# A third output row buffer, an earlier release of one weight load, and a range check moved to another place in the stream

## The chip, the cores and the metric

The kernel runs on one core of a Trainium2 chip. A core has a matrix engine (PE), whose weight loads are listed apart (PEld), a vector engine (DVE), an activation engine (ACT), a general engine (POOL) and a queue engine (SP) that mostly issues transfers. Every engine works through its own instructions in order and waits for the others by semaphores. The metric is the time of one execution in microseconds on the device, the median of several runs. A profile comes from one execution of its own.

## The reference

A gated linear attention is followed by a gated state-space layer with an output product. B, H, S, D are 4, 8, 768, 48; the model width is 384, the inner width 512.

```python
# attention, for every batch and head
for t in range(S):
    state = alpha[:, :, t, :, None] * state + einsum('bhd,bhe->bhde', k[:, :, t], v[:, :, t])
    y[:, :, t] = einsum('bhd,bhde->bhe', q[:, :, t], state)
# x: the heads side by side, (4, 768, 384)
proj = x @ w_in                       # w_in is 384 x 1024, float64 in memory
val, gate = proj[..., :512], proj[..., 512:]
for t in range(S):
    h = exp(A_log)[0] * h + val[:, t, :]      # one factor per channel in the kernel
    ys[:, t, :] = h
out = (gate * sigmoid(gate) * ys) @ w_out     # w_out is 512 x 384, float64 in memory
```

## The kernel before

The 4 x 768 steps are cut into N = 12 groups of 256, three to a batch. The kernel has two ways to compute: `fast`, which holds for inputs in a certain range, and `general`, which is correct for all. `fast` checks the range as it goes and leaves the last output product to a branch: if the check is good, the short last block (lines 1256 to 1270) makes that product, otherwise `general` starts over.

The order of the work in `fast` is written out by hand: there is no scheduler, and every engine takes its instructions in the order of the code.

The attention of a group m has these steps. `turn` or `turned` brings the raw rows of alpha, q, k into the layout needed; `scan_P` and `scan_V` make running products of alpha (DVE); `scaled_q` and `scaled_k` multiply; `scores` (PE, L792), `masks` (DVE L802 or L807, ACT, POOL); `values` (PE, L826 or, for the first group, L910), `states` (PE, L858), `carried` (PE, L839), and `join`, which copies the result out of PSUM and moves it by small transfers into xT. `first(m)` stands for scores and masks, `second(m)` for values across, states and sums, `third(m)` for carried, values and join.

The layer behind it has four projections for a group n, `project(n, cc)` with cc from 0 to 3: twelve matmul passes on PE (L976), a scan on DVE over the value half as soon as that half is there (L983), a Silu on ACT over the gate half (L994), and a product f on POOL, or on DVE in the first two and the last group (L996). Then `output(n)`: sixteen passes on PE (L1010) into two banks, of which the first is whole after fourteen; ACT copies each bank into an SBUF tile `o_sb` (L1004) taken from the pool `rows`, and SP issues its transfer to `out` (L1005). The pool has two buffers before. It belongs to the outermost function, and the last block takes its two tiles (L1267, L1269) from it as well.

The loop turn n does the projections of group n, the attention of group m = n + 1, and `output(n)` at its end. From n = 2 on, a turn's order is: `second(m)`, four projections, `third(m)`, `first(m + 1)` (there is none in turn 10, the attention being done), `output(n)`. The last turn, 11, has the four projections only, then all engines load the flag of the range check (L1234) and take the branch (L1255). A hint for the branch's target is given just before.

The weights come as float64 words and are converted on the chip. `w_in` is in four units of two transfers of 384 KB, one for each cc; `w_out` in two halves. For a unit i, `low(i)` (ACT, L543) takes the low word, `high(i)` (DVE, L549 and L551) the high word, `add_low(i)` (POOL, L556) joins them; `convert(i)` is the three together. PE's projection cc needs unit cc converted. Ahead of the loop the loads are held back by small instructions that write one element of their target: the load must wait for that write. For unit 1 it is a `memset` of DVE (L1059) that stands behind `high(0)`; for the loads after it (alpha of group 2, unit 2, and so on) it is a small copy of ACT (L1068). SP issues all of them in order.

The range check has these parts. `check_w(i)` makes the largest and the smallest absolute value of the high words of unit i (two reductions on DVE, L567), for i from 0 to 5: four units of `w_in`, two halves of `w_out`. `check_end()` (L574 to L583) turns these and the attention's own limits into one number for each partition, `okc`. `check_flag()` adds them over the partitions with a matmul into the bank s0 (L587), compares the sum (L589) and writes the integer `flag` (L590).

In turn 10 (n == N - 2), units 0 and 1 are checked behind the second projection, unit 2 behind the third, units 3 to 5 and the check's end behind `third(m)`. `check_flag()` stands in turn 11 behind the third projection.

## Time and profile before

| what | us |
|---|---|
| median of 3 runs | 276.58 |
| lowest and highest | 276.08, 277.28 |
| the profiled execution | 276.15 |
| its span, first to last instruction | 274.4 |

| engine | busy, us | share of the span |
|---|---|---|
| PE, matmul | 269.5 | 98% |
| PEld, weight loads | 216.9 | 79% |
| DVE | 217.7 | 79% |
| ACT | 109.6 | 40% |
| POOL | 123.8 | 45% |

The granted clock of PE was 1.00. A row of a timeline has the start and the length in us, the engine, the line of the kernel, the operation, output <- input, the shape, a count, and in brackets the idle time of the engine just before with what ended it. In a row of the chain of waits stand start, length and the work. Matmuls are pipelined and their ends are modelled, so the start of what waits for them is the surer mark. A letter q behind an engine's name (SPq, PEldq) is its sequencer: issues of transfers, loads of registers.

### The profile page before, as it was taken

Reading aid. Unit: us, or ns where it says so; the run is one execution under the profiler, and the core shown is the slowest. Engines: PE = TensorE matmul, PEld = TensorE weight load, DVE = VectorE, ACT = ScalarE, POOL = GpSimd, SP = SyncE. Lnnn points to the kernel's source line nnn. Section 1 sums busy time; section 2 is a strip of 40 time slices with the busy share of each in tenths; the row PEclk is TensorE's granted clock in tenths of the full one; section 3 lists DMA queues with packets and bytes.
Section 4 is the critical chain, followed back from the end, with each engine's and each line's share of the span. In section 5 each row is a group of like instructions: output and inputs, shape, how many; then the busy total and the mean of one; then the engine's idle time right before and its main releaser. Section 6 shows DMA issues by size and latency. Waiting matters only on the chain.

```text
span 274.4 us, 9649 instructions
## 1 busy us (share of the span) xinstructions
PE 269.5 (98%) x4060; PEld 216.9 (79%) x4060; DVE 217.7 (79%) x271; ACT 109.6 (40%) x252; POOL 123.8 (45%) x144
## 2 busy tenths in 40 slices
PE   8999999999999999999999999999999999999995
PEld 6988888877788687788688688688687787786874
DVE  6979998996798999694995995996995992179440
ACT  3668766451344333523434424425425415213211
POOL 8122223260137485385384485376366476325000
PEclk9999999999999999999999999999999999999999
DMA  6937985989639686774677595586596501201101
GB/s 188 319 113 221 304 182 160 256 172 230 168 92 227 163 189 152 199 170 116 153 183 155 149 210 136 142 202 144 137 210 146 137 0 36 70 0 42 63 5 60
DMA packets 52303, 41.18 MB, mean 150 GB/s; under 512 B 27392, under 2 KB 50944, under 8 KB 52256
## 3 DMA queue, kind: packets, MB, share of 16 engines
q1 hardware_dynamic: 49328, 37.34, 54.2%
q0 software_dynamic: 1536, 2.20, 2.9%
q10 hardware_dynamic: 1392, 0.99, 1.2%
q8 instruction: 33, 0.54, 0.9%
q14 instruction: 14, 0.11, 0.1%
HBM read 32.54 MB, written 4.72 MB: 136 GB/s over the span
## 4 chain that ended last, share of the span: by engine, by line
PE 91%; DVE 5%; issue 1%; ACT 1%; POOL 1%; DVEq 0%; POOLq 0%; ACTq 0%
PE mm L976 46%; PE mm L1010 21%; PE y L826 4%; PE y L839 4%; PE mm L792 3%; PE s L792 3%; PE s L858 3%; PE mm L1262 2%; DVE P L635 2%; PE mm L701 1%; PE y L773 1%; DVE V L654 1%; POOL w_in L556 1%; PE s L717 1%; DVE Zk L619 0%
## 5 line engine op out<-in xcount | busy, mean ns | idle before, releaser
L976 PE MATMUL mm<-xT,w_in 128*128 128x256 f32 x576 | 129.7, 382 | 0.1
L976 PEld LDWEIGHTS mm<-xT,w_in 128*128 128x128 f32 x576 | 107.9, 190 | 16.2 <-POOL w_in L556 0.4
L1010 PE MATMUL mm<-w_out,f_last 128*128 128x384 f32 x160 | 54.2, 492 | 0.0
L994 ACT ACTIVATE sg<-mm 128x256 f32<-128x256 f32 x48 | 18.4, 383 | 86.1 <-PE mm L976 86.0
L996 POOL TENSOR_TENSOR f_last<-sg,hh 128x256 f32<-128x256 f32 x36 | 33.0, 918 | 33.5 <-ACT sg L994 17.7
L1010 PEld LDWEIGHTS mm<-w_out,f_last 128*128 128x128 f32 x160 | 29.7, 190 | 19.8
L878 POOL TENSOR_TENSOR sum<-sum,dS 128x192 f32<-128x192 f32 x30 | 30.3, 1010 | 21.5 <-ACT dS L866 11.8
L983 DVE TENSOR_TENSOR_SCAN hh<-a_dec,hh,mm 128x256 f32<-128x256 f32 x32 | 23.4, 731 | 16.1 <-PE mm L976 16.1
L635 DVE TENSOR_TENSOR_SCAN P<-al,lower 128x1028 f32<-128x1028 f32 x12 | 31.4, 2618 | 0.5
L654 DVE TENSOR_TENSOR_SCAN V<-al,ends 128x1028 f32<-128x1028 f32 x12 | 28.3, 2360 | 0.4
L955 POOL DMA_DIRECT2D xT<-yst x44 | 22.5, 517 | 12.5 <-ACT yst L952 11.2
L1004 ACT ACTIVATE o_sb<-mm 128x384 f32<-128x384 f32 x22 | 10.8, 490 | 37.3 <-issue 21.2
L810 POOL TENSOR_TENSOR AK<-AK,mask 128x512 f32<-128x512 f32 x9 | 15.2, 1684 | 18.7 <-ACT AK L808 18.7
L807 DVE TENSOR_TENSOR A<-s,mask 128x256 f32<-128x256 f32 x9 | 3.8, 425 | 19.5 <-PE s L792 19.5
L556 POOL TENSOR_TENSOR w_in<-w_in,wr 128x768 int32<-128x768 int32 x4 | 7.3, 1822 | 25.9 <-DVE wr L551 16.1
L600 DVE STREAM_TRANSPOSE k<-raw_k 128x1024 f32<-128x1024 f32 x9 | 18.3, 2035 | 0.0
L600 DVE STREAM_TRANSPOSE q<-raw_q 128x1024 f32<-128x1024 f32 x9 | 18.2, 2021 | 0.0
L600 DVE STREAM_TRANSPOSE al<-raw_a 128x1024 f32<-128x1024 f32 x8 | 16.3, 2038 | 0.0
L619 DVE TENSOR_TENSOR Zk<-k,V 128x1024 f32<-128x1024 f32 (+1 forms) x14 | 16.1, 1150 | 0.1
L826 PEld LDWEIGHTS y<-AK,v 64*64 64x64 f32 x352 | 12.1, 134 | 5.1 <-issue 5.1
L610 DVE TENSOR_TENSOR Zq<-q,P 128x1024 f32<-128x1024 f32 (+1 forms) x14 | 14.8, 1060 | 0.1
L826 PE MATMUL y<-A,v 64*64 64x64 f32 x352 | 14.5, 221 | 0.0
(163 smaller groups left out, 389.7 us busy)
## 6 DMA issues: line engine op xcount, KB each, us to landing
v<-in_v_dram SPq DMA_DIRECT2D x22, 192.0 KB, 3.3
out_dram<-o_sb SPq DMA_DIRECT2D x22, 192.0 KB, 2.2
raw_k<-in_k_dram SPq DMA_DIRECT2D x18, 184.0 KB, 3.7
raw_q<-in_q_dram SPq DMA_DIRECT2D x18, 184.0 KB, 3.8
raw_k<-in_k_dram SPq DMA_DIRECT2D x18, 176.0 KB, 3.9
raw_q<-in_q_dram SPq DMA_DIRECT2D x18, 176.0 KB, 4.0
wbits<-in_moe_w_in_dram SPq DMA_DIRECT2D x8, 384.0 KB, 5.3
raw_a<-in_alpha_dram SPq DMA_DIRECT2D x16, 184.0 KB, 4.9
```

The lines of the kernel that those rows point to most:

```text
L600: nc.vector.transpose(out=by_runs(to).rearrange("p h c j -> p h j c"), in_=raws[name][:, 0:4 * ROW].rearrange("p (h j d) -> p h j d", h=4, ...
L635: nc.vector.tensor_tensor_scan(out=P, data0=al[:, 0:4 * GP], data1=lower.rearrange("p h t -> p (h t)"), initial=0.0, op0=ALU.mult, op1=ALU ...
L654: nc.vector.tensor_tensor_scan(out=V[:, ::-1], data0=al[:, 1:4 * GP + 1][:, ::-1], data1=ends.rearrange("p h t -> p (h t)")[:, ::-1], init ...
L792: nc.tensor.matmul(scs[m][c][i][ds(L * h, L), ds(p * (L + D), L + D)], Zk[rows, c, p, ds(h * L, L)], Zq[rows, u, p], start=True, stop=True ...
L826: nc.tensor.matmul(ys[m][i][ds(64 * s, 64), e, ds(c * C + h * L, L)], v_sb[rows, c, 4 * i + p, :], As[i][rows, c, p, :], start=across and ...
L878: nc.gpsimd.tensor_add(Ss[j][:, :, 0:D], Ss[j - 1][:, :, 0:D], part)
L955: engines[n % len(engines)].dma_start(out=xT[to, a], in_=st[rows, i, e])
L976: nc.tensor.matmul((pv, pg)[vg], w_ins[cc][:, kk, vg, :], xT[:, kk, :], start=(kk == 0), stop=(kk == NK - 1))
L983: nc.vector.tensor_tensor_scan(out=hh, data0=a_dec[:, cc:cc + 1].to_broadcast([C, GC]), data1=pv, initial=prev_h[cc][:, GC - 1:GC] if n % ...
L994: nc.scalar.activation(sg, pg, AF.Silu)
L996: f = lambda: engine.tensor_mul(fs[n][cc], sg, hh)
L1010: nc.tensor.matmul(os[c], fs[n][cc][:, ds(c * C, C)], w_outs[cc // 2][:, cc % 2, :], start=(cc == 0), stop=(cc == NI - 1))
```

## The change

There are three edits.

1. The pool `rows` has three buffers in place of two.
2. The `memset` that holds the load of unit 1, and the load's two transfers on SP, stand ahead of `low(0)` and `high(0)`, right behind `masks(0)`. On DVE the memset now precedes the two instructions of `high(0)`; on SP the order of issues is the same.
3. The parts of the range check stand elsewhere. In turn 10, units 0 to 3 are checked ahead of the first projection's scan, unit 4 behind the second, unit 5 behind the third, and the check's end behind the fourth. `check_flag()` comes at the end of turn 10 ahead of `output(10)`: on PE its matmul stands between the last matmuls of `third(11)` (L839) and the first of `output(10)` (L1010), and on DVE the two instructions of the flag precede the scans of turn 11.

The number of instructions is the same on every engine. The waits that are built into them differ in a few places: the copies into `o_sb` wait for a transfer one output further back, and L587 now has a wait for DVE (okc).

```diff
@@ ahead of the loop
     masks(0)
+    nc.vector.memset(wbits[units[1]][0:1, 0, 0, 0:1, 0], 0)
+    load_w(units[1], nc.sync)
     low(0)
     high(0)
-    nc.vector.memset(wbits[units[1]][0:1, 0, 0, 0:1, 0], 0)
-    load_w(units[1], nc.sync)
     add_low(0)
@@ the loop, n of 2 and more
+            if n == N - 2:
+                for i in range(4):
+                    check_w(i)
             f0 = project(n, 0)
             f0()
...
             if n == N - 2:
-                for i in range(0, 2):
-                    check_w(i)
+                check_w(4)
             go(1)
             f2 = project(n, 2)
             f2()
             if n == N - 2:
-                check_w(2)
-            if n == N - 1:
-                check_flag()
+                check_w(5)
...
             f3 = project(n, 3)
             f3()
+            if n == N - 2:
+                check_end()
             third(m)
...
         if n == N - 2:
-            for i in range(3, NW):
-                check_w(i)
-            check_end()
+            check_flag()
...
@@ the outermost function
-    rows = ctx.enter_context(tc.tile_pool(name="rows", bufs=2))
+    rows = ctx.enter_context(tc.tile_pool(name="rows", bufs=3))
```

## The prediction

> **What bounds the kernel now.** I read the page's engine shares first, then the busy time in two stretches, then the chain of waits at the end, and last the timelines of the single engines around the three edits.

> ```profile
> PE 269.5 (98%) x4060; PEld 216.9 (79%) x4060; DVE 217.7 (79%) x271; ACT 109.6 (40%) x252; POOL 123.8 (45%) x144
> ```
> ```profile
> 27.67:271.10 243.43, 243.33 (x3550) 194.12 (x3550) 194.14 (x224) 92.20 (x212) 113.33 (x126) 1.00 0.59 144
> 16.00:27.67 11.67, 11.55 (x306) 10.03 (x304) 10.29 (x16) 8.72 (x20) 3.64 (x2) 1.00 0.63 196
> 16.00:17.40 1.40, 1.40 (x56) 1.20 (x58) 1.30 (x4) 1.38 (x3) 0.00 (x0) 1.00 0.04 12
> ```

> The columns behind the length are the busy times of PE, PEld, DVE, ACT and POOL, then the granted clock (1.00, so no row is slowed by it), the DMA share and GB/s. PE is idle for 243.43 - 243.33 = 0.10 us between 27.67 and 271.10, and for 11.67 - 11.55 = 0.12 us in the stretch before. From 16 us on the time is PE's own work. An edit can win only by taking instructions or breaks out of PE's stream, and it can lose only by making PE wait. PE's busy time is modelled, so I check it with the start times of other engines below.

> The chain that ended last, over the end of the kernel (start, length, what):

> ```profile
> 58.87 5.16 PE mm L1010 x16
> ...
> 249.18 0.70 PE y L839 x48
> 249.88 5.36 PE mm L1010 x16
> 255.24 7.77 PE mm L976 x36
> 263.01 0.12 PE s L587 x2
> 263.13 2.79 PE mm L976 x12
> 265.92 5.19 PE mm L1262 x24
> ```

> There is no hole in it. Three projections take 7.77, or 2.59 each; the one behind the check's sum (L587) takes 2.79. Likewise L1010 takes 5.16 behind a projection and 5.36 behind the small matmuls of L839. So PE pays 0.20 for the first large matmul behind a small one.

> **The change, part by part.**

> *1. The sum of the check (L587).* Its place in PE's stream moves from between two projections of the last turn to between L839 (249.18) and L1010 (249.88) of the turn before. What it costs today, read from DVE, whose scans start when PE has finished a group:

> ```profile
> 259.16 0.75 DVE L983 TENSOR_TENSOR_SCAN hh<-a_dec,hh,mm 128x256 f32<-128x256 f32 x1 [0.40 <-PE mm L976]
> 261.75 0.75 DVE L983 TENSOR_TENSOR_SCAN hh<-a_dec,hh,mm 128x256 f32<-128x256 f32 x1 [0.40 <-PE mm L976]
> ...
> 264.66 0.75 DVE L983 TENSOR_TENSOR_SCAN hh<-a_dec,hh,mm 128x256 f32<-128x256 f32 x1 [0.48 <-PE mm L976]
> ```

> From scan to scan it is 261.75 - 259.16 = 2.59 without the sum and 264.66 - 261.75 = 2.91 with it: 0.32, which is its own 0.12 and the 0.20 of the next large matmul. At the new place the next large matmul is L1010, which pays its 0.20 already. So I expect 0.12 there instead of 0.32: -0.20. No row shows a sum behind L839, so I bound it. At best it hides wholly among L839's small matmuls (-0.32). At worst it costs its old 0.32 and another 0.12 for a break between it and L839 (+0.12). I take -0.20, because both of its pieces come from this chain.

> *2. The check's reductions and whether the sum must wait.* PE works in order: if okc is late, L587 holds L1010 and everything behind it. That is the one wait the change adds to the path.

> ```profile
> 231.13 0.42 DVE L807 TENSOR_TENSOR A<-mm,mask 128x256 f32<-128x256 f32 x1 [0.34 <-PE mm L792]
> 239.37 0.75 DVE L983 TENSOR_TENSOR_SCAN hh<-a_dec,hh,mm 128x256 f32<-128x256 f32 x1 [7.81 <-PE mm L976]
> 241.96 0.75 DVE L983 TENSOR_TENSOR_SCAN hh<-a_dec,hh,mm 128x256 f32<-128x256 f32 x1 [1.84 <-PE mm L976]
> 242.62 0.93 DVE L567 TENSOR_REDUCE wmax<-wbits 128x1 f32<-128x768 f32 x1
> ...
> 244.33 0.94 DVE L567 TENSOR_REDUCE wmax<-wbits 128x1 f32<-128x768 f32 x1
> ...
> 248.41 0.74 DVE L983 TENSOR_TENSOR_SCAN hh<-a_dec,hh,mm 128x256 f32<-128x256 f32 x1
> ...
> 254.20 0.18 DVE L574 TENSOR_SCALAR rok<-ratio 128x48 f32<-128x48 f32 x1
> ...
> 255.10 0.16 DVE L583 TENSOR_REDUCE okc<-ok 128x1 f32<-128x4 f32 x1
> ```

> One reduction follows the other after (244.33 - 242.62) / 2 = 0.855, and a scan holds DVE for 242.62 - 241.96 = 0.66 before the next instruction. The first eight (four units, largest and smallest) now go ahead of the first scan, into DVE's hole of 7.81 us: from 231.56 they take 6.84 and end at 238.40, 0.97 before that scan can start, so it stays at 239.37. The scans that follow can start no sooner than 2.59 apart, PE's pace: 241.96, 244.55 and 247.14. Two reductions go behind the second scan (242.62 to 244.33) and two behind the third (245.21 to 246.92), each pair inside its gap. The last scan moves up from 248.41 to 247.14. The check's end takes 255.10 + 0.16 - 254.20 = 1.06 from 247.80, so okc stands at 248.86. PE comes to the sum at 249.88: 1.02 to spare. The cost is 0. If the cover were gone, PE would wait for every microsecond beyond it. POOL's products behind the last two scans only get sooner.

> *3. The flag.* It is known at about 264.2 and will be at about 250.4, as soon as the sum is through and DVE has rounded it. The engines load it behind their own last work; PE's load and the first weight load past the branch:

> ```profile
> L1234 PEldq TENSOR_LOAD <-flag x1: 489/489/489, 264.2 to 264.2; - x1
> ```
> ```profile
> 265.54 5.26 PEld L1262 LDWEIGHTS mm<-w_out,f_last 128*128 128x128 f32 x24
> ```

> PE's sequencer ran ahead and waited for the flag at 264.2; its matmuls meanwhile ran on to 265.92 without a hole. So the earlier flag gives 0 on PE's path. Bounds: 0, and 0.49 of the load plus 265.54 - 264.69 = 0.85 up to the next weight load, 1.34, if some of PE's steady pace hid a delay there.

> *4. The second unit of w_in.* The one-element memset that holds its load goes ahead of high(0).

> ```profile
> 16.23 0.55 DVE L549 TENSOR_SCALAR w_in<-wbits 128x768 uint32<-128x768 uint32 x1
> ...
> 17.25 0.06 DVE L1059 MEMSET wbits<- 1x1 uint32 x1
> 18.37 0.36 DVE L927 TENSOR_TENSOR wide_S<-s,wide_S 128x192 f32<-128x192 f32 x1 [1.06 <-ACT wide_S L925]
> ...
> 24.58 0.55 DVE L549 TENSOR_SCALAR w_in<-wbits 128x768 uint32<-128x768 uint32 x1
> ```
> ```profile
> 17.36 0.91 SPq L454 DMA_DIRECT2D wbits<-in_moe_w_in_dram  x2
> 20.10 2.07 SPq L422 DMA_DIRECT2D raw_a<-in_alpha_dram  x2
> ```
> ```profile
> 16.57 1.10 ACT L543 ACTIVATE wr<-wbits 128x768 uint16<-128x768 uint32 x1
> ...
> 19.89 0.18 ACT L1068 ACTIVATE raw_a<-sum 1x1 f32<-1x1 f32 x1
> ...
> 23.22 1.07 ACT L543 ACTIVATE wr<-wbits 128x768 uint16<-128x768 uint32 x1
> ```

> The memset moves from 17.25 to about 16.25, so SP issues the two loads of 384 KB about 1.0 sooner, into a stretch in which the DMAs are 4% busy. SP passes nothing: its next issue waits for ACT's marker at 19.89 and stays at 20.10. The first reader is low(1) at 23.22, which follows its predecessor on ACT without a wait; high(1) at 24.58 follows DVE's own scans. So nobody waits for this load today. high(0) comes 0.06 later, under DVE's idle 1.06 before 18.37 and under low(0), which ends at 17.67 and for which add_low(0) waits too. 0, with a bound from:

> ```profile
> 27.67 2.46 PEld L976 LDWEIGHTS mm<-xT,w_in 128*128 128x128 f32 x12 [0.36 <-POOL w_in L556]
> ```

> That 0.36 is all that PE waits for the converted second unit; taken away wholly it would give -0.36. On the loss side the 0.06, uncovered, is the price.

> *5. The third row buffer.* An output row tile is written once more after two, now three, others.

> ```profile
> 235.88 0.49 ACT L1004 ACTIVATE o_sb<-mm 128x384 f32<-128x384 f32 x1 [3.06 <-issue]
> ...
> 254.68 0.49 ACT L1004 ACTIVATE o_sb<-mm 128x384 f32<-128x384 f32 x1 [2.96 <-issue]
> ```
> ```profile
> out_dram<-o_sb SPq DMA_DIRECT2D x22, 192.0 KB, 2.2
> ```

> A buffer's turn comes after 254.68 - 235.88 = 18.80, and its transfer lands in 2.2. The copy starts when its fourteenth of sixteen matmuls is through: 249.88 + 0.20 + 14 x 5.16 / 16 = 254.60. The transfer holds nothing: 0. The two transfers of the last turn sit behind the same rule with more room.

> Sum: -0.20 + 0 + 0 + 0 + 0. The profiled execution took 276.15 with a span of 274.4, so 1.75 lies around it; it becomes 275.95. The median of the runs, 276.58, lies 0.43 above the profiled one, and from it the sum gives 276.38. I say 276.3.

> **The rivals.**

> *The sum stops PE (slower).* Place: L587 in front of L1010. It decides from okc later than 249.88. After the second scan's end at 242.62 the order is two reductions, a scan's 0.66, two reductions, a scan's 0.66 and the 1.06: 242.62 + 2.38 + 4r, which passes 249.88 at r = 1.22, that is 1.43 times today's 0.855. If the reductions ran at twice their time (r = 1.71), okc would come at 251.84: PE waits 1.96, and with -0.20 the time is 276.58 + 1.76 = 278.3. For it: DVE can be slowed by its neighbours, since one product (L619) takes 2.57 beside POOL and another of its size (L610) 1.21:

> ```profile
> 26.13 2.57 DVE L619 TENSOR_TENSOR Zk<-k,V 128x1024 f32<-128x1024 f32 x1
> 28.62 1.21 DVE L610 TENSOR_TENSOR Zq<-q,P 128x1024 f32<-128x1024 f32 x1
> ```

> Against it: between 242.62 and 244.33 the reductions keep their 0.855 though POOL works from 243.70.

> ```profile
> 243.70 0.73 POOL L996 TENSOR_TENSOR f_last<-sg,hh 128x256 f32<-128x256 f32 x1 [1.87 <-ACT sg L994]
> ```

> [...]

> *The branch was not free (faster).* If PE's passage of the branch hides a delay that the modelled ends don't show, the flag 14 us sooner takes it out: up to 1.34, with -0.20 a time of 276.58 - 1.54 = 275.0. For it: PE did wait for the flag at 264.2. Against it: 265.92 + 8 x 5.16 / 16 = 268.50, and ACT copies the first row at 268.67, as a stream without a break would have it. [...]

> *The start was bound by the load (faster, but little).* If the second unit's conversion comes sooner, PE saves at most 0.36 at 27.67: 276.58 - 0.56 = 276.0. Against it: high(1) waits for DVE's scans, not for the data.

> *Two of the three edits do nothing.* That is part of the forecast: buffer and load release waits that no row shows.

> **How the numbers follow.** Forecast 0.70, start 0.09, branch 0.12, stopped sum 0.09. A measurement of this kernel tells about 0.5% (1.38 us) from no change. Forecast and start lie within it: 0.79. The branch gives faster, 0.12; the stop gives slower, 0.09. The range reaches down to 275.3, below the start case reckoned from the profiled run (275.6) and into the smaller sizes of the branch case; up to 277.0, the worst of part 1 from the median (276.7) and the scatter of the runs (276.08 to 277.28). Only the full branch and the stop lie outside. The likeliest case's own range is 275.9 to 276.8.

> **What would show it.** Right: eight reductions between 231.5 and 238.5, okc at about 248.9, L587 at about 249.9 with no idle time of PE before it, scans of the last turn 2.59 apart all through, and the last block starting about 0.2 sooner; the loads at about 16.4 on SP and low(1) still at 23.2. Wrong: an idle time of PE in front of L587 (the stop); the last block's first matmul sooner by over 0.5 (the branch); project(0, 1) starting sooner than 27.6 (the load); or any row far from these places that has changed its length.

## The result and the profile after

| | before | changed |
|---|---|---|
| median, us | 276.46 (7 runs) | 279.54 (7 runs) |
| lowest and highest | 275.92, 277.28 | 277.64, 279.73 |
| the profiled execution, and its span | 276.15, 274.4 | 279.56, 277.8 |
| its granted clock of PE | 1.000 | 0.994 |

The ratio is 1.0089 with a 95% interval of 1.0062 to 1.0117: the changed kernel is slower by 0.9%. Ratios, here and below, leave out executions that lie more than 1.5% above the fastest of their kernel. Its seven runs fall into two groups: three of 277.64 to 278.31 with a granted clock of 1.000, and four of 279.54 to 279.73 with 0.994.

The page of the changed kernel, its engine shares, and PE's busy share and granted clock in 40 slices:

```profile
PE 271.1 (98%) x4060; PEld 217.8 (78%) x4060; DVE 218.1 (79%) x271; ACT 109.7 (39%) x252; POOL 124.2 (45%) x144
...
PE   8999999999899999999999999999999999999995
...
PEclk9999999999979999999999999999999999999999
```

The shares look as before, and PE is still 98% busy. Two signs are new on PE: the 8 in the eleventh slice of its own row (69.5 to 76.4 us), and the 7 of its clock in the twelfth (76.4 to 83.3 us). The chain of waits of the changed kernel, around these slices and at the end (start, length, what):

```profile
71.85 0.93 PE s L792 x32
...
73.62 0.41 DVE A L807
74.02 1.09 DVE P L635
...
76.14 0.73 DVE hh L983
...
76.92 5.84 PE mm L976 x18
...
83.39 0.72 PE s L858 x64
...
90.81 0.77 PE s L792 x32
...
253.47 0.12 PE s L587 x2
253.59 5.36 PE mm L1010 x16
258.95 10.36 PE mm L976 x48
269.31 5.19 PE mm L1262 x24
```

The chain, which ran through PE alone before, now leaves it at 73.62 and goes over DVE: a mask (L807), the long scan of the attention (L635), then the scan of a projection (L983); PE's next matmul starts right behind that one. It is `project(2, 0)`, far from every line of the diff. The same place in the timelines of PE after, PE before, and DVE before:

```profile
73.48 1.56 PE L976 MATMUL mm<-xT,w_in 128*128 128x256 f32 x6
76.92 5.84 PE L976 MATMUL mm<-xT,w_in 128*128 128x256 f32 x18 [1.88 <-DVE hh L983]
```
```profile
73.41 5.45 PE L976 MATMUL mm<-xT,w_in 128*128 128x256 f32 x24
```
```profile
73.87 2.29 DVE L635 TENSOR_TENSOR_SCAN P<-al,lower 128x1028 f32<-128x1028 f32 x1
76.07 0.72 DVE L983 TENSOR_TENSOR_SCAN hh<-a_dec,hh,mm 128x256 f32<-128x256 f32 x1
```

A projection is six matmuls for the value half and six for the gate half, and the scan L983 reads the value half. Before, the 24 matmuls of two projections ran through. Now PE stops after the first six, until L983 has read them. That scan was just as late before (76.07), behind the same L635; nobody waited for it then. The stretches around the stop, in the changed kernel (columns as in the prediction):

```profile
75.00:76.00 1.00, 0.04 (x1) 0.00 (x0) 1.00 (x1) 0.00 (x0) 1.00 (x1) 1.00 0.04 9
76.00:77.00 1.00, 0.08 (x1) 0.08 (x1) 1.00 (x3) 0.00 (x0) 1.00 (x1) 1.00 0.00 0
77.00:78.00 1.00, 1.00 (x4) 0.86 (x5) 1.00 (x1) 0.00 (x0) 0.28 (x1) 0.76 0.00 0
78.00:79.00 1.00, 1.00 (x4) 0.82 (x3) 0.94 (x3) 0.00 (x0) 0.00 (x0) 0.50 0.00 0
...
80.00:81.00 1.00, 1.00 (x4) 0.82 (x3) 1.00 (x1) 0.87 (x2) 1.00 (x1) 0.54 0.89 282
```

PE is idle from 75.04 to 76.92, and 0.6 us after it has started again the granted clock falls to 0.50. In steps of 0.2 us it reads 1.00 up to 77.40, 0.78 in the next, 0.50 from 77.60 to 80.80, 0.69 in the next and 1.00 from 81.00 on. Taking it to change from 1.00 straight to 0.50 and back, the means of 0.76 and 0.54 above put the fall at 77.52 and the return at 80.92: by this estimate 3.40 us at one half.

The loss, by the chains. L858 starts at 83.39 and started at 79.48: +3.91. Of that, +0.07 was there before the place (L792 at 71.85, before at 71.78). The idle time is 1.88. The 18 matmuls take 5.84; at full clock behind the same pause they take 4.15 (second experiment), so the clock is 1.69, which is what 3.40 us at one half come to (1.70). In a steady stream, at 2.59 for twelve, they would take 3.88; the 0.27 from there to 4.15 is put down to starting the stream anew: twelve behind a pause take 2.86 in place of 2.59 (84.58 in the sixth experiment), also 0.27 more. 0.07 + 1.88 + 0.27 + 1.69 = 3.91.

What comes back later is 0.52. The check's sum is 0.20 (below). The other 0.32 is a small stop that the chain of before had here, and which is gone:

```profile
86.90 0.09 issue
86.99 1.00 PE s L792 x32
```

0.09 and 1.00 have become the 0.77 at 90.81. In all 3.91 - 0.52 = 3.39, and the spans differ by 3.4.

The check in the changed kernel, in DVE's timeline:

```profile
235.06 0.96 DVE L567 TENSOR_REDUCE wmax<-wbits 128x1 f32<-128x768 f32 x1
...
241.08 0.95 DVE L567 TENSOR_REDUCE wmin<-wbits 128x1 f32<-128x768 f32 x1
242.96 0.75 DVE L983 TENSOR_TENSOR_SCAN hh<-a_dec,hh,mm 128x256 f32<-128x256 f32 x1 [0.92 <-PE mm L976]
...
252.26 0.16 DVE L583 TENSOR_REDUCE okc<-ok 128x1 f32<-128x4 f32 x1
```

The eight reductions are (241.08 - 235.06) / 7 = 0.86 apart and end 0.92 before the scan can start. okc is there at 252.42, 1.05 before PE comes to L587 at 253.47, without a break. From L1010 on the chain of before had 5.36 + 7.77 + 0.12 + 2.79 = 16.04; now it is 0.12 + 5.36 + 10.36 = 15.84.

Why PE waits for the scan stands in the program as built. The first wait of the gate half of `project(2, 0)` has another engine (an excerpt of the two lists of PE's instructions with their waits; before with -, changed with +):

```
-L976 Matmult mm<-xT,w_in_93 128x256 [waits Activation_49]
+L976 Matmult mm<-xT,w_in_93 128x256 [waits DVE_49]
```

`bank_pair()` asks the pool `ps_mm` for two tiles, the value half and the gate half, and the pool has four PSUM banks. In the program of before it hands out bank 2 and bank 3 here. In the changed program both tiles lie in bank 2: the gate half may be written only when the scan has read the value half out of it. It is the first tile of this pool, the 48th, that the two programs place differently. All this is read from the built programs, as no trace names a bank; the trace shows only that L983 ends PE's wait. So the question for the runs was which edit does this, and whether the shared bank is the whole price.

### The profile page after: what moved, and what is told of

The parts are those of the page before. It is cut to its first block, busy times and chain, and to the rows that moved or that the text cites. A ratio compares the mean times of both kernels' runs of the same rounds, so it can differ in the third digit from the quotient of the medians.

```text
span 277.8 us, 9640 instructions
## 1 busy us (share of the span) xinstructions
PE 271.1 (98%) x4060; PEld 217.8 (78%) x4060; DVE 218.1 (79%) x271; ACT 109.7 (39%) x252; POOL 124.2 (45%) x144
## 4 chain that ended last, share of the span: by engine, by line
PE 89%; DVE 5%; issue 2%; ACT 1%; DMA 1%; POOL 1%; DVEq 0%; ACTq 0%; POOLq 0%
PE mm L976 45%; PE mm L1010 21%; PE y L826 4%; PE y L839 4%; PE mm L792 3%; PE s L792 3%; PE s L858 3%; DVE P L635 2%; PE mm L1262 2%; PE mm L701 1%; DMA raw_a<-in_alpha_dram 1%; DVE V L654 1%; POOL w_in L556 1%; PE s L717 0%; DVE Zk L619 0%
## 5 line engine op out<-in xcount | busy, mean ns | idle before, releaser
L976 PE MATMUL mm<-xT,w_in 128*128 128x256 f32 x576 | 131.4, 386 | 2.0 <-DVE hh L983 1.9
L976 PEld LDWEIGHTS mm<-xT,w_in 128*128 128x128 f32 x576 | 109.1, 192 | 18.9 <-DVE hh L983 2.3
L1010 PE MATMUL mm<-w_out,f_last 128*128 128x384 f32 x160 | 54.2, 492 | 0.0
L994 ACT ACTIVATE sg<-mm 128x256 f32<-128x256 f32 x48 | 18.4, 384 | 90.4 <-PE mm L976 90.3
L996 POOL TENSOR_TENSOR f_last<-sg,hh 128x256 f32<-128x256 f32 x36 | 32.3, 899 | 35.1 <-ACT sg L994 27.6
L1010 PEld LDWEIGHTS mm<-w_out,f_last 128*128 128x128 f32 x160 | 29.7, 190 | 19.7
L878 POOL TENSOR_TENSOR sum<-sum,dS 128x192 f32<-128x192 f32 x30 | 31.4, 1045 | 21.8 <-ACT dS L866 12.1
L983 DVE TENSOR_TENSOR_SCAN hh<-a_dec,hh,mm 128x256 f32<-128x256 f32 x32 | 23.5, 734 | 15.3 <-PE mm L976 15.0
L635 DVE TENSOR_TENSOR_SCAN P<-al,lower 128x1028 f32<-128x1028 f32 x12 | 31.1, 2594 | 0.5
L1004 ACT ACTIVATE o_sb<-mm 128x384 f32<-128x384 f32 x22 | 10.8, 491 | 37.1 <-PE mm L1010 37.1
L807 DVE TENSOR_TENSOR A<-s,mask 128x256 f32<-128x256 f32 x9 | 3.8, 424 | 22.2 <-PE s L792 22.2
L556 POOL TENSOR_TENSOR w_in<-w_in,wr 128x768 int32<-128x768 int32 x4 | 7.3, 1822 | 25.8 <-DVE wr L551 16.1
L619 DVE TENSOR_TENSOR Zk<-k,V 128x1024 f32<-128x1024 f32 (+1 forms) x14 | 16.1, 1149 | 0.1
L610 DVE TENSOR_TENSOR Zq<-q,P 128x1024 f32<-128x1024 f32 (+1 forms) x14 | 14.8, 1058 | 0.1
L839 PEld LDWEIGHTS y<-Zq,sum 48*64 48x64 f32 x656 | 11.8, 134 | 3.5 <-issue 3.2
## 6 DMA issues: line engine op xcount, KB each, us to landing
v<-in_v_dram SPq DMA_DIRECT2D x22, 192.0 KB, 3.4
out_dram<-o_sb SPq DMA_DIRECT2D x22, 192.0 KB, 2.3
```

The lines of the kernel that those rows point to most:

```text
L635: nc.vector.tensor_tensor_scan(out=P, data0=al[:, 0:4 * GP], data1=lower.rearrange("p h t -> p (h t)"), initial=0.0, op0=ALU.mult, op1=ALU ...
L839: nc.tensor.matmul(ys[m][i][ds(64 * s, 64), e, ds(u * L, L)], Ss[j][rows, p, :], Zqs[m % 2][rows, u, p, D:], start=False, stop=True, skip_ ...
L878: nc.gpsimd.tensor_add(Ss[j][:, :, 0:D], Ss[j - 1][:, :, 0:D], part)
L976: nc.tensor.matmul((pv, pg)[vg], w_ins[cc][:, kk, vg, :], xT[:, kk, :], start=(kk == 0), stop=(kk == NK - 1))
L983: nc.vector.tensor_tensor_scan(out=hh, data0=a_dec[:, cc:cc + 1].to_broadcast([C, GC]), data1=pv, initial=prev_h[cc][:, GC - 1:GC] if n % ...
L994: nc.scalar.activation(sg, pg, AF.Silu)
```

## The experiments

Each run was compared with runs of the kernel before on the same chip, listed beside it. "Low clock" counts the executions whose mean granted clock was under 0.996.

| run | median, us (runs) | before | ratio (95%) | low clock |
|---|---|---|---|---|
| e1_rows3 | 279.70 (4) | 276.23 | 1.0101 (1.0069 to 1.0134) | 3 of 4 |
| e2_one_bank | 278.90 (4) | 276.23 | 1.0101 (1.0066 to 1.0135) | 2 of 4 |
| e3_banks_kept | 276.05 (12) | 276.23 | 0.9998 (0.9975 to 1.0022) | 1 of 12 |
| e4_rows2 | 276.18 (12) | 276.23 | 1.0009 (0.9984 to 1.0035) | 1 of 12 |
| e5_filled | 277.98 (8) | 276.16 | 1.0080 (1.0049 to 1.0111) | 1 of 8 |
| e6_scan_first | 277.49 (12) | 276.16 | 1.0050 (1.0019 to 1.0082) | 2 of 12 |
| e7_check | 275.99 (10) | 276.16 | 0.9994 (0.9966 to 1.0022) | 0 of 10 |
| e8_load | 276.29 (10) | 276.16 | 0.9997 (0.9979 to 1.0014) | 2 of 10 |
| e9_load_again | 276.35 (12) | 276.21 | 1.0018 (0.9986 to 1.0049) | 2 of 12 |
| e10_check_again | 275.88 (12) | 276.21 | 0.9985 (0.9965 to 1.0005) | 0 of 12 |

The kernel before, in the same sessions: none of 76. Three of its executions lie at 279.1 to 279.6 all the same, at full clock, so a long execution alone proves nothing.

### The third row buffer alone

```diff
-    rows = ctx.enter_context(tc.tile_pool(name="rows", bufs=2))
+    rows = ctx.enter_context(tc.tile_pool(name="rows", bufs=3))
```

> The kernel before with the third row buffer alone. Theory A (bank sharing): in the program built with three row buffers, the two halves of project(2, 0) get the same PSUM bank, so the gate half must wait for the scan of the value half, which stands on DVE behind scan_P(4). Expected: PE idle for about 1.9 us at 75 to 77, the scan at about 76.1, span about 276 where the clock holds and about 278 where it falls after the pause; time 1.4 to 3.5 us above before. Theory B (the stop at the check's sum costs the time): no change against before, within 0.4 us.

Measured: 279.66, 279.73 and 279.87 at a clock of 0.994, 278.10 at 1.000. Its chain of waits has the stop at the same place:

```profile
76.07 0.73 DVE hh L983
...
76.84 5.84 PE mm L976 x18
```

With the other two edits absent the loss is whole: +3.47 in the medians, +1.87 in the run with full clock. It comes from this edit.

### The shared bank alone

Before with its two row buffers, and the banks written out by hand, in the order of before, except that the gate half of `project(2, 0)` gets the bank of its value half (the "22" in the string).

```diff
+    banks = iter("0321032103231023102310231023102310231023102310220123102310321032103210320132013201230123012301320132013201230123012301320132013201230123012301320132012301230123")
...
-        return ps_mm.tile([C, 512], FP32, tag="mm", name="mm")
+        return ps_mm.tile([C, 512], FP32, tag=f"mm{next(banks)}", name="mm")
...
-    ps_mm = ctx.enter_context(tc.tile_pool(name="ps_mm", bufs=4, space=bass.MemoryType.PSUM))
+    ps_mm = ctx.enter_context(tc.tile_pool(name="ps_mm", bufs=1, space=bass.MemoryType.PSUM))
```

The three tiles of the last block (L1260) get the tags mm0 to mm2.

> The kernel before, two row buffers, with its PSUM banks written out by hand in the order that it has, save one: the gate half of project(2, 0) is put into the bank of its value half. Theory A: the same pause of about 1.9 us and 1.4 to 3.5 us above before, without any third buffer. Theory C (the third buffer costs by itself, by its waits or by moving the other tiles in SBUF): no change against before, within 0.4 us.

Measured: 277.42 and 277.96 at full clock, 279.83 and 279.84 at 0.994. The profiled execution is one of the first two. Its chain, and its stretches:

```profile
75.50 0.73 DVE hh L983
...
76.28 4.15 PE mm L976 x18
```
```profile
75.00:76.00 1.00, 0.00 (x0) 0.00 (x0) 1.00 (x2) 0.00 (x0) 1.00 (x1) 1.00 0.00 0
...
77.00:78.00 1.00, 1.00 (x6) 0.87 (x6) 1.00 (x1) 0.12 (x1) 0.00 (x0) 1.00 0.00 0
```

Two row buffers, none of the three edits, and the loss is there with both of its sizes. One tile's bank makes it. The profile also shows the pause, again 1.88 us long, without the fall of the clock: the same 18 matmuls in 4.15 in place of 5.84.

### All three edits with the banks of before

The same edit of the pool on the changed kernel, with "23" where the string above has "22".

> The changed kernel, all three edits, with the PSUM banks written out by hand in the order of the kernel before. Theory A: no pause at 75 us; what is left is the prediction's 0.20 at the check's sum, so 0 to 0.4 us below before. Theories B and C: 1.4 to 3.5 us above before, as the changed kernel is.

```profile
74.48 5.38 PE mm L976 x24
```

The 24 matmuls of turn 2 run through in 5.38, as in the chain of before, and the median is back at 276.05, though the third row buffer is in. So the buffer by itself costs nothing that the times can show; what it costs is the banks. One execution in twelve still was at 279.45, with a clock of 0.993.

### The changed kernel with two row buffers

```diff
-    rows = ctx.enter_context(tc.tile_pool(name="rows", bufs=3))
+    rows = ctx.enter_context(tc.tile_pool(name="rows", bufs=2))
```

> The changed kernel with two row buffers: the check's new place and the earlier load, nothing else. Theory A: as e3, 0 to 0.4 us below before, okc at about 248.9 and the sum at about 249.9 without a pause of PE. Theory B: still 1.4 to 3.5 us above before. Theory C: as theory A here.

```profile
73.77 5.38 PE mm L976 x24
```

276.18 against 276.23: without the third buffer the other two edits make no difference that the times can show. The stop is gone; a gain of 0.20 in 276 lies inside the interval.

### The pause filled

Is it the idle time that lowers the clock? The changed kernel, with four matmuls of zeros between the two halves of `project(2, 0)`, which nobody reads. The wait and its length stay, PE works through most of it.

```diff
-            f0 = project(n, 0)
+            f0 = project(n, 0, between=(lambda: keep_warm(4, 256)) if n == 2 else None)
```

> The changed kernel with four extra matmuls on zeros (1.7 us of PE work, their result is not used) between the value half and the gate half of project(2, 0), that is in the pause. The gate half still waits for the scan, so the pause itself costs its 1.9 us. Theory A1 (the granted clock falls because PE stood idle): the clock stays 1.00 in all runs, and all runs lie 1.2 to 2.0 us above before, none at 3 and more. Theory A2 (the fall of the clock has another cause, as the bank or the moment): some runs are still 3 us and more above before with a clock of 0.994, as in the changed kernel.

Its chain and its stretches:

```profile
76.10 0.73 DVE hh L983
...
76.88 4.15 PE mm L976 x18
```
```profile
75.00:76.00 1.00, 1.00 (x6) 0.86 (x6) 1.00 (x1) 0.00 (x0) 1.00 (x1) 1.00 0.06 20
76.00:77.00 1.00, 0.86 (x5) 0.43 (x4) 1.00 (x3) 0.00 (x0) 1.00 (x1) 1.00 0.00 0
```

Seven of eight executions lie between 277.29 and 278.53 at a clock of 0.998 or more; one, at 280.96 and 0.993, missed the expectation and has no profile. With the pause unfilled a low clock came in nine of fifteen (changed kernel, first and second experiment).

The one looks like another kind, by its size. The nine lie 1.6 to 2.2 us above the median of their kernel's executions at full clock, which fits the 1.69 of the fall. The one lies 3.0 above, and the low-clock executions of the kernels without the stop (third and fourth experiment, and the earlier load alone) lie 2.9 to 4.0 above theirs. So a fall of the stop's size came in nine of fifteen with PE idle and in none of eight with PE at work, which supports that the idle time lowers the clock. The waiting itself costs 277.98 - 276.16 = 1.82 all the same.

### The scan taken ahead of the long one

The changed kernel with its shared bank, but in turn 2 the attention's step with L635 goes behind the scan of `project(2, 0)` on DVE.

```diff
-            else:
+            elif n != 2:
                 go(1)
...
             f0 = project(n, 0)
+            if n == 2: go(1)
             f0()
```

> The changed kernel with the same banks, but in turn 2 the scan of project(2, 0) stands ahead of scan_P(4) on DVE. If the gate half waits for that scan alone, the pause shrinks from about 1.9 us to the scan's 0.75 and a start of 0.1 to 0.2, about 0.9: 0.5 to 1.0 us above before, with little or no fall of the clock. scan_P(4) and what follows it on DVE come about 1.6 later, which may add to this. If the pause comes from something else than the scan, it stays at 1.9 us and the time at 1.4 to 3.5 above before.

Its stretches, and its chain:

```profile
75.00:76.00 1.00, 0.16 (x2) 0.05 (x1) 0.84 (x2) 0.00 (x0) 0.61 (x1) 1.00 0.02 8
76.00:77.00 1.00, 1.00 (x5) 0.90 (x6) 1.00 (x1) 0.00 (x0) 0.00 (x0) 1.00 0.00 0
```
```profile
75.82 2.27 DVE P L635
...
83.78 0.75 DVE hh L983
...
84.58 2.86 PE mm L976 x12
```

The first pause shrinks from 1.88 to 0.84 and the clock holds behind it in this execution. What I had not reckoned with is the second half: L635 now starts at 75.82 in place of 73.94, all of DVE's work behind it is late, and a later L983 at 83.78 stops PE once more, for 0.34. So +1.33 in place of the 0.5 to 1.0 expected. The length of the pause follows DVE's order, as the theory says; the order cannot repair it.

### The check's new place alone, twice

```diff
+            if n == N - 2:
+                for i in range(4):
+                    check_w(i)
             f0 = project(n, 0)
...
-                for i in range(0, 2):
-                    check_w(i)
+                check_w(4)
...
             if n == N - 2:
-                check_w(2)
-            if n == N - 1:
-                check_flag()
+                check_w(5)
...
+            if n == N - 2:
+                check_end()
             third(m)
...
-            for i in range(3, NW):
-                check_w(i)
-            check_end()
+            check_flag()
```

> The kernel before with the check's new place alone (two row buffers, load as before). By the prediction's first term: 0.20 shorter on PE's stream, the sum in front of L1010 at about 249.9 with no pause before it, 10.36 for the four projections of the last turn in one piece. Time 0 to 0.4 us below before; by the rival of the stopped sum up to 1.8 above.

> e7 once more beside e9, for the count of executions with a fallen clock and for the size of the gain. Time 0 to 0.4 us below before; under D2 no execution 3 us above before, under D1 as many as in e9.

The chain of the first, and one row of its DVE timeline:

```profile
249.66 0.12 PE s L587 x2
249.78 5.36 PE mm L1010 x16
255.14 10.36 PE mm L976 x48
```
```profile
248.45 0.16 DVE L583 TENSOR_REDUCE okc<-ok 128x1 f32<-128x4 f32 x1
```

The trace shows the 15.84 again, okc 249.66 - 248.61 = 1.05 ahead of PE, and no stop. The medians are 0.17 and 0.33 under those of before, and both intervals hold 1. By the chain it keeps the 0.20 and none of the stop, but the times alone do not show it faster.

### The earlier load alone, twice

```diff
     masks(0)
+    nc.vector.memset(wbits[units[1]][0:1, 0, 0, 0:1, 0], 0)
+    load_w(units[1], nc.sync)
     low(0)
     high(0)
-    nc.vector.memset(wbits[units[1]][0:1, 0, 0, 0:1, 0], 0)
-    load_w(units[1], nc.sync)
```

> The kernel before with the earlier load of the second unit alone. Expected: the load issued at about 16.4, low(1) still at 23.2 and project(0, 1) at 27.6; time within 0.2 us of before, if its spread allows to tell. By the rival of the start, up to 0.36 below.

> e8 once more, since the profile of e8 fell on an execution with two pauses of PE at 16.8 and 20.5 that no row explains, and a clock that fell after them. Theory D1 (the pauses come now and then whatever the kernel): most executions as before, load at about 16.4, low(1) at 23.2, project(0, 1) at 27.6, time within 0.2 us of before, and no more executions with a fallen clock than e10 has. Theory D2 (the earlier load brings them on): several executions of the ten or so lie 3 us and more above before with a clock of about 0.994, and e10 has none.

Medians of 276.29 and 276.35: no gain. The second one's profile, SP's timeline and the chain where the loaded unit is first used:

```profile
16.60 1.54 SPq L454 DMA_DIRECT2D wbits<-in_moe_w_in_dram  x2
```
```profile
14.76 1.06 PE mm L792 x32
...
24.91 0.46 DVE w_in L549
...
27.91 2.86 PE mm L976 x12
```

This execution is 0.24 us late before the load comes into it: L792 starts at 14.76, in the chain of before at 14.52. The load is issued at 16.60, before at 17.36, so 0.76 sooner by the clock and 1.00 against the work around it. Nothing behind it gains: from that L792, the conversion L549 follows after 10.15 in both (24.91, before 24.67), and PE's first use after 13.15 in both (27.91, before 27.67).

The profile of the first fell on an execution of 280.10 us. Its stretches near the start:

```profile
20.00:22.00 2.00, 0.51 (x18) 0.36 (x17) 1.99 (x2) 0.68 (x2) 0.00 (x0) 1.00 0.02 6
22.00:24.00 2.00, 1.85 (x69) 1.85 (x70) 1.90 (x4) 0.00 (x0) 0.00 (x0) 0.71 0.84 227
```

PE stands idle for 1.65 us around 21, after a first pause of 0.60 at 16.75, and the granted clock falls behind it, to a mean of 0.71. No engine releases either pause; the chain calls them "issue":

```profile
20.51 1.65 issue
```

One thing in this trace is late ahead of both. The page lists a DMA queue for instructions (q8, 33 packets). In the eleven other traces its first packet behind 8 us begins at 8.3 to 13.8 and its second at 16.0 to 18.0. Here they begin at 14.88 and 19.92, and PE goes on 1.35 and 1.27 us after they have ended. The first begins 1.37 ahead of the load's issue (16.25), so the load has not delayed that one. The kernel with the check alone, which has no earlier load, shows a pause at the same instruction (L918) in its second profile, the one with the latest second packet of the eleven (18.00; PE goes on 1.40 after its end). There the clock held:

```profile
19.88 0.48 issue
```

That PE waited for these packets is not shown, as no run varied them.

The counts point at the load. Over all kernels that hold it and run turn 2 without the stop, a low clock came 6 times in 46 (e3, e4, e8, e9); in those without the load and without the stop, 0 times in 22 (e7, e10), and 0 in 76 before. By time alone, above 279 us, it is 7 in 46 against 0 in 22 and 3 in 76. The one profile of such an execution does not bear the load out as the cause of its first pause. So between D1 and D2 it stays open whether the load makes such pauses more frequent. The one in e5 and the two in e6 (3.0 to 3.9 above the rest) may be of the same kind; both hold the earlier load.

## Why the prediction was wrong, by its own steps

1. *The sum of the check*: right, by the chain. -0.20 forecast, 16.04 to 15.84 measured, within a hundredth in every profile that has it. The times are too scattered to show it.
2. *The reductions*: right. 1.02 to spare forecast, 1.05 found; the reductions 0.86 apart, all eight through before the first scan. The rival of the stopped sum falls. The 0.86 is the same with POOL at work beside the reductions (236.18 to 238.02 in the changed kernel) and without.
3. *The flag*: right, 0. The last block follows the last projection without a hole, at 269.31 behind 258.95 + 10.36. The rival of the branch falls.
4. *The load*: 0, right as to the medians of the kernel with this edit alone. PE's first use moves no sooner. Rare executions with a low clock were not foreseen; whether the load makes them more frequent is not settled.
5. *The third row buffer*: this is the step that failed. It said that "buffer and load release waits that no row shows" and priced the buffer by the output's transfer alone: "The transfer holds nothing: 0." About the transfer that was right (third experiment: 276.05 with three buffers). But it took for granted that the pool of row buffers touches nothing else. In the program as built, one more buffer there changes the banks that `ps_mm` hands out from turn 2 on, and one pair gets a single bank. The price is 1.88 of idle time, 0.27 for the new start and, in nine executions of fifteen, 1.69 by the clock; 0.32 of it comes back at the next attention step.

The rows for it were on hand: L635 holds DVE from 73.87 to 76.16 in the trace of before, so any matmul tied to the scan behind it would be some 1.9 us late. Missing was the tie, and that stood in the waits of the built program. The description of the change names the waits of the copies into `o_sb` and of L587 as those that differ; that list was too short, since the wait of L976 in turn 2 belongs on it. Of the prediction's signs, the last one caught it: a row far from the edits that changed its length.

The range went wrong with the step: it bounded the known terms and the scatter (275.3 to 277.0) and held no term for a rearranged pool. All four of its rivals sat at the edits' own lines.

Still open is why the pool takes another bank when another pool has one more buffer. That it does was read from the built programs (three row buffers alone do it, the load alone and the check alone do not), and the traces agree: the stop is in e1 and not in e4, e7, e8, e9 or e10. The rule by which it chooses was not tried.

## What to carry to other kernels

After any change of a pool, compare the waits of every instruction in the two built programs, not only those at the edited lines; a wait that has changed engines is priced by what that engine is doing then. Where two tiles must be written one after the other and read by different engines, give each a bank by name instead of leaving it to a pool. The share of 98% busy hid the stop of 1.88 us in 277.8: look at the chain for a step that leaves the bound engine.
